# The last row of w_out, loaded in one DMA or in 16 pieces of 15 to 1 partitions

## The chip, the cores and the metric

The kernel runs on one core of a Trainium2 chip. The metric is the device time of one execution in microseconds; lower is better. The median of three runs of the kernel before is 132.11 us (132.06 to 132.54).

A core has a matrix engine (PE; its weight loads are listed as PEld), a vector engine (DVE), a scalar engine (ACT), GpSimd (POOL) and a sync engine (SP), each with its own instruction stream, and 16 DMA engines. A DMA is issued by an instruction in the stream of one engine. In the profile a name with a q (SPq, ACTq) is the sequencer of an engine, which waits and issues.

## The reference

One decode step of a layer with two parallel branches on one token (D = 576): an attention over a cache, of which the last W = 4096 positions count, and a gated MLP. All data are bfloat16.

```python
x  = A_x                                    # [1, 1, 576]
xn = _layernorm(x)

# branch A: 32 query heads, 16 key/value heads, head size 128
q = (xn @ wq)                               # [32, 128]
k, v = k_cache[:, :, Sk-W:], v_cache[:, :, Sk-W:]
o = softmax(q k^T * Dh**-0.5) v
a = o.reshape(4096) @ wo                    # wo: [4096, 576]

# branch B: Fh = 2304
z = gelu(xn @ w_in)                         # w_in: [576, 4608]
z1, z2 = z[..., :Fh], _layernorm(z[..., Fh:])
g = w_sp * z2 + b_sp                        # one position: w_sp and b_sp are single numbers
b = (z1 * g) @ w_out                        # w_out: [2304, 576]

return x + a + b
```

All inputs that the computation touches are read once, 51 MB in all: the last 4096 positions of k and v (16 heads each, 1 MB per head), wq, wo, w_in and w_out.

## The kernel before

**Loads.** Every large load is issued from SP, in one fixed order written at the top of the kernel, ahead of all computing: two heads of k, wq, and then per pair of heads the next k, the v of the pair before, and a part of w_in or wo (lines 104 to 116). The load of w_out comes last (line 117). `load_kv` (line 79), `load_rows` (line 92) and `load_wo` (line 99) each take a tile from the pool `units`, which has 18 buffers, and issue one DMA into it. The schedule is manual: each engine runs its instructions in the order in which the code issues them. Waits are put in by the framework, from the tiles that are read and written and from the buffers that are reused. It also gives the DMAs of SP and ACT their completion counters.

**w_out.** `wout_v` (line 77) views w_out as 128 partitions of 18 rows: partition p holds the rows 18 p to 18 p + 17, each of 576 numbers (1152 bytes). Line 117 loads them in four DMAs, cut by row: rows 0 to 7 (1152 KB), 8 to 13 (864 KB), 14 to 16 (432 KB), and row 17 alone (144 KB). Each DMA has all 128 partitions. `load_rows` enters each row into `wout_t`, so that `wout_t[j]` is a [128, 576] slice.

**Computing.** Per pair of heads, PE transposes the k tiles (`T`, line 203), forms the scores (`S`, line 215), and after the softmax sums v (`PV`, line 258). Between these stand the parts of the MLP (`z_part`, line 294) and of the output projection (`WO`, line 280).

**The end.** The output row collects in one PSUM tile, `out_ps`: x, the four parts of wo, and w_out. A row of w_out takes four matmuls, one for each 144 columns (`out_mm`, line 275):

```python
    for j in range(FR):
        out_mm(hv[:, j:j + 1], wout_t[j], last=j == FR - 1)

    res = const.tile([P, OW], BF16, name="res")
    nc.vector.tensor_copy(res[0:97, :], out_ps[0:97, :])
    nc.sync.dma_start(out.flatten_outer_dims()..., res[0:97:32, :])
```

These are lines 391 to 396. `hv` (line 330), the gated hidden vector, is ready long before, so each row's matmuls need only that row's load. They are PE's last work. Then DVE copies `out_ps` to `res` (line 395), and SP issues the output DMA (line 396), the last entry in its stream.

Of the kernel before, what the change touches and what calls it, by code (L numbers as in the profile page):

```python
# [9 lines left out]
BF16 = mybir.dt.bfloat16  # L10
# [4 lines left out]
P = 128  # L15
D = 576
# [16 lines left out]
FR = FH // P  # L33
# [5 lines left out]
def kernel(  # L39
# [14 lines left out]
    nc = tc.nc  # L54
# [4 lines left out]
    units = ctx.enter_context(tc.tile_pool(name="units", bufs=UNITS))  # L59
# [13 lines left out]
    kn, vn, wq_t, win_t, wo_t, wout_t = {}, {}, {}, {}, {}, {}  # L73
# [3 lines left out]
    wout_v = B_w_out.rearrange("(p r) n -> p r n", r=FR)  # L77
# [14 lines left out]
    def load_rows(store, view, name, width, cuts):  # L92
        for a, e in zip(cuts, cuts[1:]):
            t = units.tile([P, e - a, width], BF16, name=f"{name}{a}", tag="u")
            nc.sync.dma_start(t[:], view[:, a:e, :])
            for i in range(a, e):
                store[i] = t[:, i - a, :]

    def load_wo(j):
        t = units.tile([P, 8 * D], BF16, name=f"wo{j}", tag="u")  # L100
        nc.sync.dma_start(t[:], wo_v[j])
        wo_t[j] = t
# [4 lines left out]
    for b in range(1, NB + 1):  # L107
# [6 lines left out]
            load_rows(win_t, win_v, "win", FH, win_parts[b])  # L114
        elif b < 7:
            load_wo(b - 4)
    load_rows(wout_t, wout_v, "wout", D, (0, 8, 14, 17, 18))


    ident = const.tile([P, P], BF16, name="ident")  # L120
# [306 lines left out]
```

## Time and profile before

| | |
|---|---|
| median of 3 runs | 132.11 us |
| the profiled execution, its own time | 131.92 us |
| its span, first to last instruction | 130.1 us |
| PE / PEld / DVE / ACT busy, share of the span | 82% / 77% / 40% / 22% |
| mean granted PE clock | 0.712 |
| the SP and ACT DMAs (queue q1): packets, bytes, share of 16 engines | 7208, 50.96 MB, 94.7% |
| HBM read | 50.96 MB, 392 GB/s over the span |
| chain that ended last, by engine | DMA 45%, PE 44%, DVE 6% |

How to read it. The span is taken from the profile of one execution; its own time is 1.8 us longer than the span. Busy shares are means over the whole span; PE and the DMA engines are both busy in most of it, so which of them bounds a stage has to be read from the stage. The chain that ended last goes back from the last instruction to whatever released it, step by step. An issue on SP has a length of its own (about 0.33 us for a load of 128 partitions), and a time from issue to landing that is mostly the queue of earlier loads ahead of it (some 20 us in the middle of the kernel). Times in the text are microseconds from the start of the span.

### The profile page before, as it was taken

How to read it: one execution, taken by the hardware profiler on the slowest of the kernel's cores; microseconds unless marked ns; L12 is line 12 of the kernel's file. 1: busy time of each engine (PE TensorE's matmuls, PEld its weight loads, DVE VectorE, ACT ScalarE, POOL GpSimd, SP SyncE). 2: the span in 40 equal slices, each digit the busy share in tenths (PEclk: the TensorE clock that was granted, in tenths of full speed). 3: DMA queues.
4: the chain of work that ended last, by engine and by line, in shares of the span. 5: the costliest groups of instructions: out<-in, count | busy, mean ns of one | idle time of the engine just before them, and what ended most of it. 6: DMA issues, size and time to landing. Idle time of an engine off the chain costs nothing.

```text
span 130.1 us, 4613 instructions
## 1 busy us (share of the span) xinstructions
PE 106.3 (82%) x2133; PEld 100.7 (77%) x2133; DVE 51.9 (40%) x157; ACT 29.2 (22%) x38; POOL 0.7 (1%) x6
## 2 busy tenths in 40 slices
PE   3589518699899998989978798799899949994790
PEld 3489418499898997989977797699779939993780
DVE  4486000355402552054436624455444552454200
ACT  3136000033200360013604060233214401340000
POOL 2000000000000000000000000000000000000000
PEclk9999655556855599555995555557977985699559
DMA  4999999999999999999999999999999999999940
GB/s 116 420 431 431 420 412 422 418 420 429 411 415 420 421 416 419 413 415 418 423 415 418 424 425 408 430 411 420 418 422 412 420 421 416 415 420 417 388 158 0
DMA packets 7232, 51.24 MB, mean 394 GB/s; under 512 B 813, under 2 KB 942, under 8 KB 1454
## 3 DMA queue, kind: packets, MB, share of 16 engines
q1 hardware_dynamic: 7208, 50.96, 94.7%
q8 instruction: 16, 0.26, 0.8%
q14 instruction: 2, 0.02, 0.0%
q10 hardware_dynamic: 6, 0.00, 0.0%
HBM read 50.96 MB, written 0.00 MB: 392 GB/s over the span
## 4 chain that ended last, share of the span: by engine, by line
DMA 45%; PE 44%; DVE 6%; issue 1%; ACT 1%; ACTq 0%; SPq 0%
DMA k<-in_A_k_cache_dram 19%; PE tp L203 18%; DMA wout<-in_B_w_out_dram 14%; DMA wq<-in_A_wq_dram 12%; PE zp L294 8%; PE s L215 6%; PE o L258 5%; PE bc L234 2%; PE out_ps L277 1%; DVE m L227 1%; PE su L249 1%; PE tr L225 1%; PE op L268 1%; DVE mb L236 1%; ACT p L241 0%
## 5 line engine op out<-in xcount | busy, mean ns | idle before, releaser
L203 PE MATMUL tp<-ident,k 128*128 128x128 bf16 x512 | 53.0, 275 | 1.3 <-DMA k<-in_A_k_cache_dram 0.8
L203 PEld LDWEIGHTS <-k 128*128 128x128 bf16 x512 | 43.9, 128 | 2.7 <-issue 1.6
L207 DVE COPY kT<-tp 128x1024 bf16<-128x1024 bf16 x40 | 27.5, 690 | 23.5 <-PE tp L203 23.5
L205 ACT COPY kT<-tp 128x1024 bf16<-128x1024 bf16 x24 | 24.3, 1011 | 34.4 <-PE tp L203 34.4
L215 PE MATMUL s<-q_bf,kT 128*128 128x2 bf16 x512 | 21.0, 166 | 1.5 <-DVE kT L207 1.4
L215 PEld LDWEIGHTS <-kT 128*128 128x128 bf16 x512 | 19.9, 103 | 1.9 <-DVE kT L207 1.6
L258 PE MATMUL o<-p,v 128*128 128x2 bf16 x512 | 15.3, 164 | 0.1
L258 PEld LDWEIGHTS <-v 128*128 128x128 bf16 x512 | 14.4, 98 | 0.2 <-issue 0.2
L241 ACT ACTIVATE p<-d 128x128 bf16<-128x128 f32 x8 | 2.5, 310 | 49.9 <-DVE d L239 49.9
L294 PEld LDWEIGHTS <-win 128*128 128x128 bf16 x162 | 10.5, 162 | 1.6 <-issue 1.6
L294 PE MATMUL zp<-xe,win 128*128 128x2 bf16 x162 | 10.4, 200 | 1.1 <-DVE m L227 1.1
L338 PE MATMUL q_ps<-xe,wq 128*128 128x2 bf16 x144 | 4.5, 165 | 4.6 <-DMA wq<-in_A_wq_dram 4.6
L338 PEld LDWEIGHTS <-wq 128*128 128x128 bf16 x144 | 4.1, 101 | 4.9 <-DMA wq<-in_A_wq_dram 4.8
L234 PEld LDWEIGHTS bc<-dg,ones_f 4*128 4x128 f32 x16 | 3.2, 244 | 5.5 <-DVE dg L229 4.3
L234 PE MATMUL bc<-dg,ones_f 4*128 4x4 f32 x16 | 3.9, 309 | 4.0 <-DVE dg L229 3.1
L277 PE MATMUL out_ps<-wo,oP 128*1 128x144 bf16 x128 | 4.3, 296 | 1.8 <-DVE oP L273 1.6
L249 PEld LDWEIGHTS su<-ss,ones_f 128*128 128x128 f32 x16 | 4.3, 328 | 1.5 <-DVE ss L244 1.5
L249 PE MATMUL su<-ss,ones_f 128*128 128x4 f32 x16 | 4.4, 343 | 1.3 <-DVE ss L244 1.3
L220 DVE TENSOR_REDUCE mx<-s 128x4 f32<-128x128 f32 x8 | 2.3, 292 | 6.8 <-PE s L215 6.8
L277 PEld LDWEIGHTS <-oP 128*1 128x1 bf16 x128 | 2.9, 106 | 2.2 <-DVE oP L273 1.8
L244 DVE TENSOR_REDUCE ss<-p 128x4 f32<-128x128 bf16 x8 | 2.3, 286 | 3.2 <-ACT p L241 3.2
L340 DVE CAST q_bf<-q_ps 128x32 bf16<-128x32 f32 x1 | 0.3, 301 | 8.2 <-PE q_ps L338 8.2
(78 smaller groups left out, 41.3 us busy)
## 6 DMA issues: line engine op xcount, KB each, us to landing
k<-in_A_k_cache_dram SPq DMA_DIRECT2D x16, 1024.0 KB, 19.4
v<-in_A_v_cache_dram SPq DMA_DIRECT2D x16, 1024.0 KB, 20.6
win<-in_B_w_in_dram SPq DMA_DIRECT2D x4, 1152.0 KB, 18.9
wo<-in_A_wo_dram SPq DMA_DIRECT2D x4, 1152.0 KB, 20.6
wq<-in_A_wq_dram SPq DMA_DIRECT2D x4, 1024.0 KB, 10.9
wout<-in_B_w_out_dram SPq DMA_DIRECT2D x1, 1152.0 KB, 20.4
wout<-in_B_w_out_dram SPq DMA_DIRECT2D x1, 864.0 KB, 19.6
win<-in_B_w_in_dram SPq DMA_DIRECT2D x1, 576.0 KB, 19.3
```

What stands on the lines that cost most here:

```text
L203: nc.tensor.transpose(tp[:, i, :], kn[h][:, 8 * c + i, :], ident[:])
L205: nc.scalar.copy(kT[n][:], tp[:])
L207: nc.vector.tensor_copy(kT[n][:], tp[:])
L215: nc.tensor.matmul(s_ps[b][:, i, 8 * c + t, :], lhsT=kT[n][:, t, :], rhs=q_bf[:, 2 * h:2 * h + 2], start=True, stop=True)
L220: nc.vector.tensor_reduce(out=mx[:], in_=s_ps[b][:].rearrange("p i t r -> p i r t"), axis=AXX, op=ALU.max)
L234: nc.tensor.matmul(bc[:], lhsT=ones_f[0:4, :], rhs=sm[b]["dg"][:], start=True, stop=True)
L241: nc.scalar.activation(p[:], d[:], ACT.Exp, scale=SCALE)
L249: nc.tensor.matmul(su[:], lhsT=ones_f[:], rhs=sm[b]["ss"][:].rearrange("p i r -> p (i r)"), start=True, stop=True)
L258: nc.tensor.matmul(sm[b]["o"][:, 2 * i:2 * i + 2], lhsT=vn[2 * b + i][:, t, :], rhs=p_sb[b][:, i, t, :], start=t == 0, stop=t == NT - 1)
L277: nc.tensor.matmul(out_ps[32 * g:32 * g + 1, :], lhsT=lhsT, rhs=rhs[:, OW * g:OW * (g + 1)], start=start, stop=last, tile_position=(0, 32 ...
L294: nc.tensor.matmul(zp[:, c, :], lhsT=w_r[:, c, :], rhs=xe_of(r), start=(r == rows.start and c == 0), stop=r == rows.stop - 1, skip_group_c ...
L338: nc.tensor.matmul(q_ps[:, c, :], lhsT=wq_t[r][:, P * c:P * (c + 1)], rhs=xe_of(r), start=(r == 0 and c == 0), stop=r == NS - 1, skip_grou ...
```

## The change

Row 17 of each partition is no longer loaded by `load_rows` in one DMA of 128 partitions. A tile for it is taken from the same pool at the same place in the order, and filled by 16 DMAs on SP: of 15 partitions, of 14, and so on to 1 (15 + 14 + ... + 1 = 120), and one of the last 8. The bytes are the same, and so are the tile, the matmuls and everything else. Lines below the change move down by 7 in the changed kernel (277 becomes 284, 396 becomes 403); the new DMAs stand on its line 122.

```diff
-    load_rows(wout_t, wout_v, "wout", D, (0, 8, 14, 17, 18))
+    load_rows(wout_t, wout_v, "wout", D, (0, 8, 14, 17))
+
+    t = units.tile([P, 1, D], BF16, name="wout17", tag="u")
+    lo = 0
+    for n in list(range(15, 0, -1)) + [8]:
+        nc.sync.dma_start(t[lo:lo + n, 0, :], wout_v[lo:lo + n, FR - 1, :])
+        lo += n
+    wout_t[FR - 1] = t[:, 0, :]
```

SP's stream in the built program has 68 entries after the change and 53 before; those of the other engines have as many entries as before.

## The prediction

> **What bounds the kernel now.** I read the chain of waits first, from its end.
>
> ```profile
> 87.27 20.57 DMA k<-in_A_k_cache_dram
> ...
> 107.91 18.61 DMA wout<-in_B_w_out_dram
> ...
> 126.55 0.61 PE out_ps L277 x16
> ...
> 127.19 0.31 DVE res L395
> ```
>
> Columns are start, length, and what it is. The last 40 us are two DMA loads in a row: the kernel ends as the stream of weights ends. The load issued at 107.91 is rows 14 to 16 of w_out; it lands at 107.91 + 18.61 = 126.52. After it come 16 matmuls (four of each of the rows 14 to 17), the copy to `res` and the output DMA, which starts at 127.53. So whatever makes the last row land later than now moves the end by as much.
>
> Second, the stages of the end, to see how the stream runs out (PE, PEld, DVE, ACT and POOL busy, then the granted clock, the DMA share, GB/s).
>
> ```profile
> 120.00:122.00 2.00, 2.00 (x62) 2.00 (x63) 0.18 (x1) 0.00 (x0) 0.00 (x0) 0.50 0.97 404
> 122.00:124.00 2.00, 1.18 (x42) 1.03 (x42) 0.60 (x3) 0.00 (x0) 0.00 (x0) 0.50 0.86 349
> 124.00:126.00 2.00, 2.00 (x72) 1.80 (x64) 0.00 (x0) 0.00 (x0) 0.00 (x0) 0.50 0.48 189
> 126.00:128.00 2.00, 0.97 (x32) 0.58 (x20) 0.31 (x1) 0.00 (x0) 0.00 (x0) 0.79 0.07 23
> ```
>
> The 16 DMA engines don't finish together: from 124 to 126 a share of 0.48, some 0.48 x 16 = 7.7 engines, is still at work. An even split leaves some engines late, and a change that moves rows between engines could touch that.
>
> Third, the SP queue, which issues every load, and how long the w_out loads take from issue to landing.
>
> ```profile
> 110.39 0.33 SPq L95 DMA_DIRECT2D wout<-in_B_w_out_dram  x1
> ```
>
> ```profile
> wout<-in_B_w_out_dram SPq DMA_DIRECT2D x1, 1152.0 KB, 20.4
> wout<-in_B_w_out_dram SPq DMA_DIRECT2D x1, 864.0 KB, 19.6
> ...
> wout<-in_B_w_out_dram SPq DMA_DIRECT2D x1, 432.0 KB, 18.6
> wout<-in_B_w_out_dram SPq DMA_DIRECT2D x1, 144.0 KB, 16.5
> ```
>
> The last row (144 KB) is issued at 110.39 and lands at 110.39 + 16.5 = 126.89, 0.37 behind rows 14 to 16; the timeline has its four matmuls start at 126.91. It is ready in the queue for 16 us; its own size costs 0.37.
>
> Fourth, what holds SP back.
>
> ```profile
> SPq L396 <- DVE res L395: 14.7, 1, 14.7
> ...
> SPq L396 <- DMA v<-in_A_v_cache_dram: 2.1, 1, 2.1
> ```
>
> The output DMA, which needs `res` alone, also waited 2.1 us for a load of v. The reason stands in the built program: every DMA of a queue counts on one of eight completion counters, in turn, and may start only when the DMA eight places before it has landed. So no more than eight are in flight. This is the place that decides the change.
>
> **The change part by part.** *Removed*: one issue on SP at 110.39 (0.33 us); nothing waited for its end.
>
> *Added*: 16 issues on SP, each on the next counter. The instruction order of the built program names each wait. Piece 1 (15 partitions) waits for the same load of v as the old row did, so it goes at 110.39. Pieces 2 to 7 wait, in turn, for the next v load, the last `wo`, the two last v loads and the w_out loads of rows 0 to 7 and 8 to 13. The latter were issued at 102.94 and 105.83, so they land at 102.94 + 20.4 = 123.3 and 105.83 + 19.6 = 125.4. Up to here the cost is nothing: seven issues lie in the 14.7 us in which SP only waited for `res`, and their bytes queue behind rows 14 to 16. If that cover went, seven issues would cost 7 x 0.40 = 2.8 (price below).
>
> Piece 8 waits for the load of rows 14 to 16, which lands at 126.52. The chain shows 0.07 from a landing to the next issue (107.84 to 107.91), so piece 8 starts at **126.58**. Then SP has eight more to issue, pieces 9 to 16; their counters are those of pieces 1 to 8. Pieces 1 to 7 land within a few tenths after 126.5, behind rows 14 to 16 on their engines, before SP gets to their followers. Piece 16 waits for piece 8, which was issued eight issues earlier.
>
> *Price of an issue* (p), start to start, once no wait intervenes. No 15-partition load is in the trace, so bounds. Below: ACT's two loads of one element, 11.68 and 11.93, 0.25. Above: the output DMA of four partitions, the only small one on SP, 0.66 long, with some 0.06 to the next, 0.72. Between them a pair of whole loads on SP back to back:
>
> ```profile
> 11.68 0.21 ACTq L343 DMA_DIRECT2D ws<-in_B_w_sp_dram  x1
> 11.93 0.26 ACTq L344 DMA_DIRECT2D ws<-in_B_b_sp_dram  x1
> ```
>
> ```profile
> 19.31 0.33 SPq L95 DMA_DIRECT2D win<-in_B_w_in_dram  x1
> 19.68 0.43 SPq L81 DMA_DIRECT2D k<-in_A_k_cache_dram  x1
> ```
>
> That is 0.37 start to start, the second itself 0.43 long. Same queue, same direction, so it is the nearest row; I take **0.40**, between 0.37 and 0.43 + 0.04. Piece 16 starts at 126.58 + 8 x 0.40 = 129.78.
>
> *Price of a landing* (L) on idle engines. `x_row`, one partition of 1.1 KB, is issued at 0.73, and PE idles for it until 2.0: 1.27. The output took 0.66 + 0.8 (SP's wait for it at the end) = 1.46, written to HBM. A piece is a load, so I take **1.30**, ends 1.25 and 1.5. Piece 16 lands at 131.08.
>
> The Trainium skill, DMA: Bandwidth & Descriptors, Rules for kernel authors, speaks against this change: coalesce many small transfers, since under 64 KB one pays mostly overhead. The same page gives about 2.0 us as the fixed cost of a DMA (from GpSimd's path); by that the sum would be 0.7 higher than by my 1.30.
>
> *Moved on PE*: the last row's first weight load and matmul now wait on eight counters, not one. SP's separate semaphore wait before the output DMA took 17 ns; eight make 0.14, part of them passed before. I take 0.1, ends 0 and 0.2. Rows 14 to 16 go at 126.55 as before.
>
> *Sum*: the last row is ready at 131.08 + 0.1 = 131.18, against 126.89: **+4.29**. Everything behind it is unchanged and moves along: the four matmuls, the copy (0.31), the output DMA. That one is queued on SP behind piece 16, but SP is free at 130.2, before `res` (131.8), and its counter (piece 9) is long down. The span becomes 130.1 + 4.3 = 134.4, and the profiled execution 131.92 + 4.3 = 136.2. The runs' median, 132.11, is 0.19 above the profiled one: 132.11 + 4.3 = **136.4**.
>
> Ends: p 0.25, L 1.25, no extra wait: 126.58 + 2.0 + 1.25 = 129.83, +2.9, 135.0. p 0.72, L 1.5, 0.2: 126.58 + 5.76 + 1.7 = 134.04, +7.1, 139.3.
>
> *The rows' shares per engine*. Eight rows per engine took 0.37, so a row some 0.046. Where pieces give an engine up to 16 rows, it ends at most 0.37 later, about 127.3, long before piece 16 lands. So this costs nothing while the tail on SP is there. Moving rows off a late engine can gain no more than the last row's wait: twelve of the 16 matmuls ended 0.47 after 126.55, at 127.02, the last at 127.14, so about 0.1.
>
> The same page, section Why a DMA increments its semaphore by 16 and not by 1, says that a DMA of n partitions uses the largest number of engines up to 16 that divides n, the lowest-numbered ones. By it the first engine gets 16 rows of this load and the last none, which would spare a late engine at the high end 0.37. No row of this trace names the engines, and the bound of 0.1 stands beside it.
>
> **Rivals.** (a) *Cheap issues*: with little to write per piece SP runs near ACT's 0.25. For it: one to eight partitions instead of 128. Against: the small output DMA took 0.66 on SP. Time with p = 0.25 and the other terms as taken: 126.58 + 2.0 + 1.4 = 129.98, +3.1, 135.2. Below p = 1.3 / 8 = 0.16 the wait of piece 16 for piece 8 takes over, two landings in series: 126.58 + 2.6 + 0.1 = 129.28, +2.4, 134.5.
>
> (b) *Dear issues*: a transfer on few partitions costs SP 0.72 each. For it: the output DMA's row; `x_row` on ACT took 0.49. Against: the two `ws` loads, 0.21 and 0.26. Time: 126.58 + 5.76 + 1.4 = 133.74, +6.9, 139.0.
>
> (c) *Not slower: the tail on SP does not exist*. If SP ran through all 16 pieces from 110.39 on, they would be out by 110.39 + 6.4 = 116.8, ten microseconds before rows 14 to 16 land, and the last row would come when it does now or up to 0.1 earlier: 132.0 to 132.1. It decides if the issues are not held by the counters. For it: the bytes are the same, and the stream has a backlog of 16 us. Against: the 2.1 us that the output DMA spent on a v load, and a wait written at each piece.
>
> **How the numbers follow.** The sum as worked out, with p from 0.32 to 0.5, 135.7 to 137.3: 0.55. (a) 0.22; (b), p above 0.5, 0.17; (c) 0.06. The range 134.7 to 138.8 takes in the likeliest case whole, nearly all of (a) and most of (b). About what a measurement of this kernel can tell from no change is 0.5%, 0.66 us. All cases but (c) are slower by over that; (c) gives 0.04 for the same and, in case more hangs on the late engines than I see, 0.02 for faster.
>
> **What would show it.** In the profile after: SP issues pieces 1 to 7 spread from 110.4 to 125.5, piece 8 at 126.6 and then eight in a row with nothing between; the start-to-start time there is p. PE's wait for w_out before its last four matmuls grows from 0.02 to some 4 us, and the DMA share from 127 to 131 is almost nothing. The transposes, softmax and rows 14 to 16 stay where they are. I am wrong if SP issues all pieces before 120, if rows 14 to 16 themselves land later than 127, or if the issues at the end are apart by more than 0.72 or by a landing each.

## The result, and the profile after

The changed kernel takes 136.26 us (136.18 to 136.36), the kernel before 132.13 us beside it: ratio 1.0306, 95% interval 1.0284 to 1.0329. It is 4.1 us slower. The profiled execution has a span of 134.5 us, against 130.1.

The chain of waits of the changed kernel, from the last of the big loads on (start, length, what):

```profile
107.99 18.84 DMA wout<-in_B_w_out_dram
126.84 0.02 issue
126.86 0.27 SPq L122
127.13 0.04 issue
127.17 0.29 SPq L122
...
129.14 0.25 SPq L122
129.39 0.04 issue
129.44 1.47 DMA wout<-in_B_w_out_dram
130.91 0.20 issue
131.11 0.32 PE out_ps L284 x3
...
131.45 0.31 DVE res L402
```

Before, the landing of rows 14 to 16 was followed by PE. Now it is followed by SP: eight issues in a row (126.86 to 129.39), with 0.04 between them, then the 16th piece, from its issue at 129.44 to its landing at 130.91, and only then PE. PE's part of it, in its timeline:

```profile
131.11 0.29 PE L284 MATMUL out_ps<-wout,hv 128*1 128x144 bf16 x4 [3.70 <-DMA wout<-in_B_w_out_dram]
```

The last four matmuls start at 131.11 instead of 126.91, 4.2 later. And the stages of the end (PE, PEld, DVE, ACT, POOL, granted clock, DMA share, GB/s):

```profile
126.00:128.00 2.00, 1.19 (x36) 0.67 (x24) 0.00 (x0) 0.00 (x0) 0.00 (x0) 0.50 0.09 23
128.00:130.00 2.00, 0.00 (x0) 0.00 (x0) 0.00 (x0) 0.00 (x0) 0.00 (x0) 0.50 0.09 16
130.00:132.00 2.00, 0.29 (x4) 0.12 (x4) 0.31 (x1) 0.00 (x0) 0.00 (x0) 0.50 0.04 5
```

From 128 to 130 no engine computes, and the 16 DMA engines are busy for 9% of the time. What fills the stage is SP's issuing, which no busy column counts.

### The profile page after: what moved, and what is told of

Its sections match the earlier page's. It is cut to its first block, busy times and chain, and to the rows that moved or that the text cites. A ratio compares the mean times of both kernels' runs of the same rounds, so it can differ in the third digit from the quotient of the medians.

```text
span 134.5 us, 4631 instructions
## 1 busy us (share of the span) xinstructions
PE 104.2 (77%) x2133; PEld 98.3 (73%) x2133; DVE 51.8 (39%) x157; ACT 29.1 (22%) x38; POOL 0.7 (1%) x6
## 4 chain that ended last, share of the span: by engine, by line
DMA 76%; PE 17%; SPq 2%; DVE 2%; issue 1%
DMA k<-in_A_k_cache_dram 34%; DMA v<-in_A_v_cache_dram 16%; DMA wout<-in_B_w_out_dram 15%; DMA wq<-in_A_wq_dram 11%; PE tp L210 7%; PE zp L301 3%; PE s L222 3%; SPq L122 2%; PE o L265 1%; PE bc L241 1%; PE su L256 0%; PE q_ps L345 0%; DVE m L234 0%; PE tr L232 0%; PE out_ps L284 0%
## 5 line engine op out<-in xcount | busy, mean ns | idle before, releaser
L210 PE MATMUL tp<-ident,k 128*128 128x128 bf16 x512 | 50.4, 265 | 1.4 <-DMA k<-in_A_k_cache_dram 0.9
L210 PEld LDWEIGHTS <-k 128*128 128x128 bf16 x512 | 41.9, 123 | 2.9 <-issue 1.9
L222 PEld LDWEIGHTS <-kT 128*128 128x128 bf16 x512 | 19.1, 101 | 1.7 <-DVE kT L214 1.4
L284 PE MATMUL out_ps<-wout,hv 128*1 128x144 bf16 x72 | 2.9, 318 | 4.7 <-DMA wout<-in_B_w_out_dram 4.7
L284 PEld LDWEIGHTS <-hv 128*1 128x1 bf16 x72 | 2.1, 115 | 5.4 <-DMA wout<-in_B_w_out_dram 4.0
```

The lines of the kernel that those rows point to most:

```text
L210: nc.tensor.transpose(tp[:, i, :], kn[h][:, 8 * c + i, :], ident[:])
L222: nc.tensor.matmul(s_ps[b][:, i, 8 * c + t, :], lhsT=kT[n][:, t, :], rhs=q_bf[:, 2 * h:2 * h + 2], start=True, stop=True)
L284: nc.tensor.matmul(out_ps[32 * g:32 * g + 1, :], lhsT=lhsT, rhs=rhs[:, OW * g:OW * (g + 1)], start=start, stop=last, tile_position=(0, 32 ...
```

## The experiments

Twelve kernels, all but one (the one with fewer matmuls) computing the same result from the same loads of everything but the last rows. The edits are of the changed kernel; the spread pieces, the pieces from GpSimd and all that follow the ascending pieces are edits of the kernel before. Theory T is the prediction's: a serial run of issues on SP behind a landed load, and one landing. Rival E came out of the landing records of the changed kernel. They are the increments of each load's completion counter in the trace, and hold the time at which each DMA engine ends its share of a load; the last of each load is:

```
rows 14 to 16            126.84
piece 1, 15 partitions   127.04
piece 2, 14              127.25
piece 3, 13              127.45
piece 4, 12              127.65
piece 5, 11              127.84
piece 6, 10              128.04
piece 7, 9               128.24
```

Seven steps of 0.20: the latest engine has one row of each piece, and each takes it 0.20. In one load of 128 partitions eight rows took 0.37. So here, where one piece follows the other with nothing between, a piece costs an engine some four times a row.

### Number and shape of the pieces

**Sixteen equal pieces.**

```diff
-    for n in list(range(15, 0, -1)) + [8]:
+    for n in [8] * 16:
```

> 16 pieces of 8 partitions each instead of 15, 14, ... 1 and 8: the same number of issues, other shares per DMA engine. Theory T (the price is the serial tail on SP: nine issues from the landing of rows 14 to 16 on, and one landing): the same as the changed kernel, 136.0 to 136.5 us; piece 8 at 126.6 to 126.9, then eight issues about 0.3 us apart. Rival S (the price is in the uneven shares of the engines): moves by over 0.5 us from 136.26, since the lowest engines then get a row of every piece.

Measured 136.12 us, ratio to the kernel before 1.0306 (1.0289 to 1.0323): the same as the changed kernel. Piece 8 is issued at 126.62, the last at 129.30, in the chain of this kernel:

```profile
126.62 0.27 SPq L122
...
129.30 1.46 DMA wout<-in_B_w_out_dram
```

The uneven shares have no part in the 4.1 us.

**Seven pieces**, so that none waits for rows 14 to 16.

```diff
-    for n in list(range(15, 0, -1)) + [8]:
+    for n in [16] * 6 + [32]:
```

> The row in seven pieces: six of 16 partitions and one of 32. None of them has to wait for rows 14 to 16 to land. Theory T alone: no tail, so no more than 0.4 us over the kernel before, 132.1 to 132.5 us. Rival E (each piece costs a late DMA engine about 0.2 us of its own, as the landing records of the changed kernel look, against 0.37 us for all eight rows in one DMA): seven pieces end 7 x 0.2 = 1.4 us after rows 14 to 16, 1.0 us later than before, 133.1 to 133.5 us.

Measured 133.35 us, ratio 1.0093 (1.0078 to 1.0108). Theory T alone, at most 132.5, fails; rival E is right. The end of the chain of this kernel:

```profile
125.58 2.47 DMA wout<-in_B_w_out_dram
...
128.13 0.32 PE out_ps L284 x4
```

The last piece is issued in time, at 125.58, but lands 2.47 later, at 128.04, behind the other pieces on the late engines. This piece, of 32 partitions, gave each engine two rows, and its last landing came 0.19 behind that of the piece before (127.85): the price is one of the piece, not of the row.

**Eight pieces**, and **twelve**.

```diff
-    for n in list(range(15, 0, -1)) + [8]:
+    for n in [16] * 8:
```

> Eight pieces of 16 partitions: one piece waits for rows 14 to 16. Theory T: that piece goes at 126.6 to 126.9 us and lands 1.4 us later, 1.3 to 1.5 us over the kernel before: 133.4 to 133.7 us. Rival E (0.2 us per piece on a late engine): 126.8 + 8 x 0.2 = 128.4, 1.5 us over, 133.6 us; the two part in the run with seven pieces and in that with twelve.

```diff
-    for n in list(range(15, 0, -1)) + [8]:
+    for n in [8] * 8 + [16] * 4:
```

> Twelve pieces, eight of 8 partitions and four of 16: five pieces are issued after rows 14 to 16 land. Theory T: four issues more than with eight pieces, 4 x 0.33 = 1.3 us, so half way between eight and sixteen pieces: 134.8 to 135.2 us. Rival E: 0.2 us more per piece, 134.2 to 134.5 us.

Measured 133.55 us (ratio 1.0113, 1.0098 to 1.0128) and 135.14 us (1.0233, 1.0217 to 1.0248). Eight fits both theories, as was said. Twelve fits T (134.8 to 135.2) and not E (134.2 to 134.5). The starts of their last landings, from the two chains, eight pieces first:

```profile
126.68 1.62 DMA wout<-in_B_w_out_dram
```

```profile
128.17 1.64 DMA wout<-in_B_w_out_dram
```

Four more issues moved the last one by 1.49. From 8 pieces to 16 the time grows by 136.12 - 133.55 = 2.57, 0.32 per piece. So both costs are real, and they lie beside each other: with seven pieces the engines' 0.2 per piece sets the end (+1.2), with eight the two come to the same, and beyond that SP's 0.32 per issue sets it.

### Where the pieces stand

**Ahead of the rest of w_out.**

```diff
-    load_rows(wout_t, wout_v, "wout", D, (0, 8, 14, 17))
     t = units.tile([P, 1, D], BF16, name="wout17", tag="u")
...
     wout_t[FR - 1] = t[:, 0, :]
+    load_rows(wout_t, wout_v, "wout", D, (0, 8, 14, 17))
```

> The same 16 pieces, issued ahead of rows 0 to 16 of w_out instead of behind them. Theory T (eight counters: a load waits for the load eight places before): the tail moves with the pieces. Piece 8 waits for the last v load (120.6 us), eight more issues follow, and rows 0 to 16 are issued only at 123.4 to 124.4, into a stream that has run dry; 2.5 MB at some 415 GB/s from about 124.7 are 6.0 us, so they land at 130.7 to 131.5 and the kernel takes 136.0 to 137.0 us. Rival H (it only hurts because the pieces are last; with 2.5 MB behind them they are hidden): 132.1 to 132.6 us.

Measured 137.94 us, ratio 1.0432 (1.0399 to 1.0465): slower than with the pieces last. Rival H fails. T named the mechanism, and its size was too small by 1 us. The stages of this kernel, in the columns of before:

```profile
118.00:120.00 2.00, 0.80 (x15) 0.50 (x11) 1.08 (x5) 0.00 (x0) 0.00 (x0) 1.00 0.49 188
120.00:122.00 2.00, 1.27 (x33) 1.28 (x34) 0.47 (x2) 0.31 (x1) 0.00 (x0) 0.65 0.06 18
122.00:124.00 2.00, 1.38 (x47) 1.23 (x43) 0.46 (x3) 0.00 (x0) 0.00 (x0) 0.50 0.10 24
124.00:126.00 2.00, 1.13 (x32) 0.92 (x33) 0.15 (x1) 0.00 (x0) 0.00 (x0) 0.50 0.64 143
```

The DMA share falls to 0.06 and 0.10: the stream runs dry while SP issues, with 2.5 MB still to fetch. It begins to run dry in 118 to 120, earlier than I had reckoned, since the engines don't end the last v load together (117.12 to 120.77 in the landing records).

**One piece behind each of 16 big loads.**

```diff
...
     def load_kv(store, cache, name, h):
...
         store[h] = t
+        if pieces and spread:
+            lo, n = pieces.pop(0)
+            nc.sync.dma_start(w17[lo:lo + n, :], wout_v[lo:lo + n, FR - 1, :])
...
     for b in range(1, NB + 1):
+        spread = b >= 4
...
```

> The same 16 pieces, all on SP, one behind each of the 16 loads of k and v of the pairs 4 to 7, so that no two pieces follow each other and eight places back there is always a load of 1 MB in flight. Theory T (it is the run of issues behind a landed load that costs): no tail and no dry stream; rows 14 to 16 are last, with 16 matmuls behind them: 132.1 to 133.0 us, the upper end if each piece costs its engine 0.2 us. Rival P (16 small DMAs cost their 4 us wherever they stand): 135.5 us and more.

The pieces go into a tile of their own here, not into one of the pool.

Measured 133.19 us, ratio 1.0077 (1.0056 to 1.0098), 0.2 above T's upper end and 2.3 below rival P. The same 16 issues on the same queue cost 1.1 us here instead of 4.1. PE's last work in it:

```profile
127.66 0.65 PE L288 MATMUL out_ps<-wout,hv 128*1 128x144 bf16 x16 [0.19 <-DMA wout<-in_B_w_out_dram]
```

There is no tail; rows 14 to 16 land at 127.62. Of the 1.1 that this is later than before, 0.37 are the row's bytes, which now lie ahead of them. The rest, 0.7, goes with the pieces, but not as 0.2 on each engine that carries one. A piece of n partitions lands on n engines, by the times the same ones each time, so an engine with a row of every piece would end 16 x 0.2 = 3.2 later (an estimate), and one that carries few pieces hardly later at all. In the landing records the first engine ends rows 14 to 16 at 124.29 instead of 123.16 and the last at 127.62 instead of 126.51; of all 16, taken in order of landing, 15 are later by 1.0 to 1.4. So in the full stream a piece costs less than in the tail, and engines with few pieces seem to pay about as much as those with many. Why was not tried.

**From GpSimd, at the start.**

```diff
     make_identity(nc, ident[:])
+    t = const.tile([P, D], BF16, name="wout17")
+    lo = 0
+    for n in list(range(15, 0, -1)) + [8]:
+        nc.gpsimd.dma_start(t[lo:lo + n, :], wout_v[lo:lo + n, FR - 1, :])
+        lo += n
...
```

> The same 16 pieces from GpSimd's queue, into a tile of their own, at the start of the kernel: another set of counters, and SP's stream ends with rows 14 to 16. Theory T: no tail; rows 14 to 16 are last, with twelve matmuls and four of the row behind them: 132.0 to 132.8 us. Rival P (16 pieces cost the engines about as much wherever they are issued): 16 x 0.2 us on the lowest engine, 135 us and more.

Measured 133.59 us, ratio 1.0105 (1.0074 to 1.0136), between the two. No tail again, but rows 14 to 16 land at 127.85. Part of that is lost while the pieces are in flight; the stage from 10 to 12 in this kernel, and in the kernel before:

```profile
10.00:12.00 2.00, 1.84 (x42) 1.71 (x40) 1.23 (x3) 1.92 (x2) 1.33 (x4) 1.00 1.00 364
```

```profile
10.00:12.00 2.00, 1.95 (x28) 1.82 (x26) 1.15 (x2) 1.34 (x2) 0.00 (x0) 1.00 1.01 430
```

The engines are as busy, but move 364 GB/s instead of 430. From 8 to 14 this makes some 0.7 us. Of the 1.3 that rows 14 to 16 are later than before, another 0.37 are the row's bytes, which lie ahead of them here too; some 0.2 stays open.

### The late engines

**Ascending pieces.**

```diff
-    for n in list(range(15, 0, -1)) + [8]:
+    for n in list(range(1, 16)) + [8]:
```

> The pieces in the order 1, 2, ... 15 and 8. The same number of issues and the same shares per engine in the end, but pieces 1 to 7 are now those of one to seven partitions, so the landing records tell of the lowest engines one at a time whether they are early or late. Theory T: eight issues from the landing of rows 14 to 16 on, of 9 to 15 and 8 partitions, at 0.32 to 0.45 us each: 136.0 to 137.2 us. Rival S (uneven shares set the time): the shares are the same, so 136.2 us as well; this run is there for the engines.

Measured 136.58 us, ratio 1.0327 (1.0295 to 1.0359), as T says. The pieces of 1 to 5 partitions ended on all their engines by 124.55; in that of 6 one engine was late (126.94). The Trainium skill, DMA: Bandwidth & Descriptors, Why a DMA increments its semaphore by 16 and not by 1, has n of up to 16 partitions run on n engines, the lowest-numbered. The records agree as to the number: one landing for each partition of a piece. If the numbers are as the page says, the first five are early engines and the sixth is not. The same page, Latency and other measured facts, names engines 7 and 15 as usually slower, and lays this, as a guess, to DMAs issued from GpSimd; here the loads come from SP, and seven of the 16 were late by over 2.3 us at the last loads (126.41 to 126.74 for rows 14 to 16, the first at 123.16).

**Rows moved to the early engines**, in search of a version better than both.

```diff
-    load_rows(wout_t, wout_v, "wout", D, (0, 8, 14, 17, 18))
+    load_rows(wout_t, wout_v, "wout", D, (0, 8, 14))
+    t = units.tile([P, 4, D], BF16, name="wout14", tag="u")
+    nc.sync.dma_start(t[0:119], wout_v[0:119, 14:FR, :])
+    nc.sync.dma_start(t[119:P], wout_v[119:P, 14:FR, :])
...
```

> Rows 14 to 17 in two DMAs, one of 119 partitions and one of 9, where the kernel before cuts by rows (14 to 16, 17). No pieces, no tail. Theory L (some engines are late by 3 us, and the seven that a DMA of 119 partitions would run on are early ones): the late engines have up to 32 row shares of 0.046 us less and end with rows 8 to 13, 125.5; the early ones have 36 more, 1.7 us, and end at 125.1 to 126.1: 131.3 to 131.8 us. Rival M (a late engine is among the seven): it ends 36 x 0.046 = 1.7 us later than before, 133.7 to 133.9 us. Rival N (the split goes evenly over all engines): as before, 132.0 to 132.2 us.

Measured 136.33 us, ratio 1.031 (1.0273 to 1.0347): worse than all three. The load of 119 partitions did land on seven engines (seven landings). PE's timeline in it:

```profile
127.84 0.89 PE L282 MATMUL out_ps<-wout,hv 128*1 128x144 bf16 x24 [1.62 <-DMA wout<-in_B_w_out_dram]
...
130.91 0.65 PE L282 MATMUL out_ps<-wout,hv 128*1 128x144 bf16 x16 [2.18 <-DMA wout<-in_B_w_out_dram]
```

Rows 8 to 13, a load of 128 partitions, also came 2.3 later than the 125.45 of before. An early engine needed 4.9 us for its 17 x 4.6 KB (121.93 to 126.83), 16 GB/s, where the full stream moves 430 / 16 = 27 per engine. So such a load is slow and slows its neighbours. Two weaker forms, with five engines (125 partitions), for row 17 alone and for rows 16 and 17 (the edit of the first is shown):

```diff
-    load_rows(wout_t, wout_v, "wout", D, (0, 8, 14, 17, 18))
+    load_rows(wout_t, wout_v, "wout", D, (0, 8, 14, 17))
+    t = units.tile([P, 1, D], BF16, name="wout17", tag="u")
+    nc.sync.dma_start(t[0:125], wout_v[0:125, 17:FR, :])
+    nc.sync.dma_start(t[125:P], wout_v[125:P, 17:FR, :])
...
```

> The kernel before with its last row in two DMAs, of 125 partitions (five engines, by the records of the ascending run all early ones) and of 3. A look for a version that is better than both: the late engines carry nothing of the row. Theory L: the row lands ahead of rows 14 to 16, and its wait of 0.1 us goes: 131.9 to 132.1 us. Rival K (a load on few engines is slow and slows the others, as with 119 partitions): 133 us and more.

> As the run before, with rows 16 and 17 in DMAs of 125 and of 3 partitions, so that the late engines have 16 row shares of 0.046 us less, 0.74 us. Theory L: they end 0.37 us before rows 14 to 16 did: 131.6 to 131.9 us. Rival K (few engines are slow): 25 x 2.3 KB at the 16 GB/s per engine that the run with 119 partitions showed is 3.6 us behind 123 us, and others slowed as there: 133 to 135 us.

Measured 132.68 us (ratio 1.0035, 1.0023 to 1.0047) and 133.08 us (1.0063, 1.0045 to 1.0082). The first lies between theory L and rival K, the second at the lower end of K; both are slower than the kernel before, by less than 1%. Rows 14 to 16 in the first landed at 127.17 instead of 126.52. Why a load on few engines disturbs the others was not tried. No version tried beats the kernel before.

**Fewer instructions.**

```diff
-        for t in range(NT):
+        for t in range(0, NT, 8):
...
-                             start=t == 0, stop=t == NT - 1)
+                             start=t == 0, stop=t == NT - 8)
```

> The kernel before with 4 of the 32 matmuls per head in the sum over v: it leaves out 7/8 of that sum, 448 matmuls and as many weight loads, 896 of PE's instructions, a fifth of them. Same loads. It asks where the late DMA engines come from. Theory F (each 16 KB packet of the instruction queue makes the engine that carries it 1.5 us late; 16 packets in the kernel before): 13 packets, and 4 or 5 engines late by 3 us at the end in place of 7; the mean engine ends 3 x 1.5 / 16 = 0.3 us earlier, the latest about as before, so 131.7 to 132.1 us. Rival G (the lateness belongs to the engines or to the loads): 7 late engines as before.

Measured 132.04 us, ratio 0.999 (0.9978 to 1.0002). The instruction queue in the kernel before, and in this one:

```profile
q8 instruction: 16, 0.26, 0.8%
```

```profile
q8 instruction: 13, 0.21, 0.7%
```

13 packets in place of 16, and at the last load 4 engines late by over 2.3 us in place of 7; in the other kernels whose stream didn't run dry, all with 16 packets, it was 7 or 8. Theory F holds, rival G does not; the run has fewer matmuls too, but the last section counts the packets against the late engines one by one. The time did not move, since the latest engine is still 3.2 us behind the first and the kernel ends with it.

## Why the prediction was right

The forecast was 136.4, in a range of 134.7 to 138.8; it took 136.26. The mechanism is shown by number (8, 12, 16 pieces) and by place (ahead of w_out, spread). Its terms were off by more than the sum, and cancelled: that the last row's matmuls were ready within 0.1 of the forecast is luck; that the tail is there and has these parts is not.

| term | forecast | measured |
|---|---|---|
| piece 8 issued | 126.58 | 126.86 |
| eight issues, each | 0.40 | 0.32 (129.44 - 126.86 = 2.58) |
| landing of piece 16 | 1.30 | 1.47 |
| PE's wait on eight counters | 0.1 | 0.20 |
| last row's matmuls ready | 131.18 | 131.11 |

- *The issue's price* is where I was furthest off, 8 x 0.08 = 0.62 too much. The nearest row by queue was a load of 128 partitions. The length of an issue goes with the size of the piece: 0.25 with one or two partitions, 0.27 to 0.29 with 8, up to 0.38 with 15 in the ascending run. Rival (b), 0.72, fell with it: the output DMA takes 0.61 here too, so that length is not what a small load costs. Rival (a), 0.25, was about as near as my own value.
- *The landing* of 1.30 was 0.17 short. By the 2.0 of the Trainium skill, DMA: Bandwidth & Descriptors, Anatomy of one DMA, it would have been 0.53 too long; the measurement decides. The upper end of 1.5 rested on a misread row: the output DMA landed 1.65 after its issue by the records (127.53 to 129.18), not 1.46.
- *Rows 14 to 16* landed 0.32 later than before, at 126.84, and piece 8 followed 0.02 behind, not 0.07. With other pieces in their place it was 126.56 to 126.74, so perhaps only part of it belongs to the change.
- *Pieces 1 to 7* do hide, but the reason I gave was wrong. I had the pieces end on the engines "at most 0.37 later, about 127.3" and "long before piece 16 lands". They end at 128.24, 0.2 per piece and not 0.046 per row. This cost nothing because the tail was longer still. Rival (c) was mispriced for the same reason: had SP been free to run ahead, 16 pieces queued at the end would by that price have taken no less than the 133.35 us of seven, not 132.0 to 132.1. That is an estimate; no run had SP free.
- *The late engines*, which I bounded at a gain of 0.1, gave none in any form that was tried.
- *A slip*: with p from 0.32 to 0.5 the sum comes to 135.8 to 137.2, not 135.7 to 137.3. Nothing hangs on it.

## What to carry to other kernels

Count the completion counters before a load is cut up: with eight, the last of nine DMAs in a row can't be issued before the first has landed. So of a run of small DMAs at the end of a stream, those from the eighth on were issued after the stream, at 0.3 us apiece, and a run ahead of the last loads drained it. Small DMAs queued one behind the other also cost each engine they use some 0.2 us; spread through a full stream, 16 of them still cost 0.7 us beyond their bytes. And a cost that is hidden should be priced all the same: here the hidden one was 1.2 us, and would have come out as soon as the larger was mended.

## What the runs showed of the hardware

The late engines come with the instruction fetches. In the kernel before, the trace has 16 packets of 16 KB on the instruction queue, each some 1.1 us long, the first at 16.05, 24.49, 32.42 and 38.54 us. The landing records of the loads around them:

```
first landing   last after it   engines late by over 0.9   over 2.3
 15.16          0.31             0                          0
 17.64          1.65             1                          0
 26.37          1.68             2                          0
 34.42          1.78             3                          0
 39.40          1.82             4                          0
 76.53          3.32             9                          1
123.16          3.35            10                          7
```

After each packet one more engine is some 1.5 us late, and from about 77 us on some are late twice. At the last row of the table one engine is late once (1.6) and seven are late twice (3.1 to 3.35): 15 in all, and 15 of the packets had started by then. The two others counted there are 1.0 late, and fell behind after two packets of 8 KB on a second instruction queue, q14, at 52.95 and 108.90. With fewer matmuls the same load has four engines late once and four twice, 12 in all, after 12 packets. Since the queue never empties they stay late, up to 3.3 us at the end, which is the DMA share of 0.48 from 124 to 126 in the prediction's stages. Where the stream ran dry (the pieces ahead of w_out), the engines ended the last load within 0.6 us of each other. That fewer instructions make fewer late engines was tried; that the packet and the late engine are the same one each time is inferred from the times, since the records don't name the engine.
